# First pair of a recurrent cross attention with a gated MLP: steps 4 to 27 reordered, the next tile's integers behind the sine, its distance behind the gate product, the first layer one step ahead

## The chip, the cores and the metric

The kernel runs on one core of a Trainium2 chip. That core has five engines which run their own instruction queues in order and wait for each other by semaphores: TensorE (matrix products, PE in the profile, PEld for its weight loads), VectorE (DVE), ScalarE (ACT), GpSimd (POOL), and SyncE (SP), which here only issues DMA transfers. The metric is the device time of one execution in microseconds, the median of several runs.

## The reference

Eight batches of an attention block feed a two-layer network. All computation is in 32-bit floats; the weights arrive as 64-bit floats and are converted in the kernel.

```python
# x: (8, 8, 512, 64), state: (8, 8, 32, 64)
scores = scale * np.matmul(x, state.transpose(0, 1, 3, 2))
a = softmax(scores);   xread = np.matmul(a, state)
scores2 = scale * np.matmul(state, x.transpose(0, 1, 3, 2))
a2 = softmax(scores2); sread = np.matmul(a2, x)
y = np.concatenate([xread, sread], axis=2)
x = y.transpose(0, 2, 1, 3).reshape(8 * 544, 512)
h = x @ w_in                 # w_in 512 x 2048
g = h * np.cos(h)
out = g @ w_out              # w_out 2048 x 512
```

## The kernel before, in words

The time axis of the program is a list of tiles (`all_tiles`, from `tiles()`), and one tile is handled in one **step**. A tile is 128 of the 2048 columns of the hidden layer for the 512 tokens of one batch; so a batch has NF = 16 tiles, a pair of batches PERIOD = 32. Steps 0 to 27 go through `first_pair`, all others through `later_pair`. The order of instructions on every engine is the order in which these functions write them (`tc.manual_schedule()`); there is no planner.

A tile goes through five stages, each with a line of its own in the profile:

- `hidden` (L493): two products of 128x512 on TensorE (four matrix instructions in the trace) fill one of two PSUM banks. The bank is free again once the tile two before it has been through its last stage. The weights of this layer are the product of the attention's state and w_in, which is why the attention's read never appears as a matrix of its own: `products` (L328) forms it for four tiles at a time, and `products_kept` (L464, ScalarE) copies it to `sw`.
- `gate` (L563): ScalarE rounds the hidden value to **integers**.
- `gate2` (L566): VectorE takes the **distance** from them.
- `gate3` (L569): ScalarE takes the **sine** of that, which is the cosine of the hidden value.
- `gate4` (L583): VectorE multiplies it with the hidden value, the **gate product**, and writes it to a slot of `g_all`, which is kept in quads of four tiles. `quads_free` lists the quads that may be written.

The second layer of the first batch is `first_product` and `second_product` (`product`, L637): tile i's gate product times a 128x256 block of w_out, at step 4 + i for the first eight tiles and at every second step from 13 on for the other eight. Their sums are taken out of PSUM by `keep_bank` (L602, ScalarE) and `plus` (L606, VectorE) with the last product of each.

Between these stages every step has other work of the same engines. It is listed by `plan(b)` in six lists, of which the step's part is `todo[0]` to `todo[5]`, and written by `go(n)`: `go(0)` on TensorE, `go(1)` and `go(2)` on ScalarE, `go(3)` and `go(4)` on VectorE, and `go(5)` for the exponentials of a block after the first two. In steps 0 to 15 it is the attention of batch 1, in steps 16 to 31 that of batch 2: turns of the tokens (L287 and L296, later L310), scores (L328), maxima (L341, L357), spreads (L347), shift (L362), exponentials (L366, L373, with a table load before and after), norm (L402), turns (L408, L413), reads (L428) and their keeping (L438, L444, L449).

Three more kinds of work are tied to the steps:

- `convert(i, parts)` turns 64-bit weights into 32-bit ones, one load of 1 MB in the steps listed in `conv_at` (0 to 8 and 11 to 15): part 1 (L243) and 2 (L246) on ScalarE, b (L249) and c (L252) on VectorE, d (L257) on GpSimd; f issues a later load (L212) on SP's queue.
- `weights_at` and `idle_at` hold sums of quarters of w_out for the faster products of all later batches: `weight_sum` (L1119, VectorE), `pool_sum` (L1155) and `inner_weights` (L684, GpSimd), which are sent to DRAM on SP's queue (`send_raw`, L672, and `send`, L687) and fetched again into a ring of four blocks (`fetch_block`, L703).
- `outer_at` and `mid_at` hold differences of gate products between the batches of a pair (`outer_sum`, `sub`, L712), on VectorE or GpSimd; `Product.sums` (L712) and `sw_sums` (L526) on GpSimd prepare the later products (`Product.stage`, L765) and the later hidden layers (`seven_part`, L543).

In `first_pair` the five stages of one tile are written in one step, with the other work between them:

```python
hidden(t); go(0); gate(t); gate2(t); go(1); go(3)
gate3(t); go(5); gate4(t); go(2); go(4)
```

so that on ScalarE a tile's sine stands behind its integers and whatever `go(1)` adds, and on VectorE its product behind its distance and whatever `go(3)` adds. The products of the second layer are written at the end of the step.

Of the kernel before, what the change touches and what calls it, by code (L numbers as in the profile page):

```python
# [13 lines left out]
ALU = mybir.AluOpType  # L14
# [8 lines left out]
def kernel(  # L23
# [616 lines left out]
    def first_product(pr, i):  # L640
        product(a11, g_all[:, QT * quads_of[0, 0][i // QT] + i % QT], i)
        if i == NH - 1:
            pr.u = Held()
            for ch in range(2):
                keep_bank(pr.u, ch)

    def second_product(pr, i):
        product(a12, g_all[:, QT * quads_of[0, 1][i // QT] + i % QT], i)
        if i == NH - 1:
            o = Held()  # L650
            for ch in range(2):
                plus(o, ch, acc[ch], pr.u)
            store(2 * pr.n, 0, o)

# [253 lines left out]
    def tiles():  # L908
        pr = None
        for b in range(B):  # L910
            if b % 2 == 0:
                pr = Pair(b // 2)
            for f in range(NF):
                t = Tile()
                t.b, t.f, t.pair = b, f, pr
                t.phase, t.i = b % 2 * 2 + f // NH, f % NH
                t.row = pr.n, t.phase
                t.n, t.kn = S, 2
                t.paired = b > 1
                t.at = 1 - f // 2 % 2  # L920
                c = slice(P * f % WC, P * f % WC + P)
                t.lhs = lambda i, b=b, nt=P * f // WC, c=c: (
                    sw_of[b, nt][:, i, c])
                t.rhs = lambda i, b=b: aT_of[b][:, i]
                yield t
# [52 lines left out]
    def plan(b):  # L978
# [57 lines left out]
        if b == 0:  # L1036
            pe[0].append((0, "products", 0, SIDE, HC, WC))
            y_dve[0] += [(0, "products_taken", 0, SIDE, HC, WC),
                         (0, "inverse2")]
            prod(7, 0, 2, SIDE)  # L1040
            prod(11, 0, 3)
            prod(13, 1, 0, SIDE)
# [21 lines left out]
    for i, t in enumerate(all_tiles):  # L1064
        t.mate = all_tiles[i ^ 1]
    pairs = [all_tiles[2 * NF * n].pair for n in range(B // 2)]
    stage_at, sums_at, outer_at, mid_at, weights_at = [
        defaultdict(list) for _ in range(5)]
    idle_at = defaultdict(list)
# [26 lines left out]
    for n in range(B // 2):  # L1096
        end = n == B // 2 - 1
        for r, engine, o, x1, x2, half in (
                ((25, 26), dve, 0, 2, 0, 0),
                ((27, 28) if n else (25, 25), dve if n else pool, 0, 2, 0, 1),  # L1100
                ((31, 31), pool, 2, 3, 2, 0), ((33, 33), dve, 0, 3, 0, 0),
# [4 lines left out]
            for i in range(2):  # L1106
                at_ = (mid_at if n == 0 and r[0] == 25 and engine is dve
                       else outer_at)
                at_[PERIOD * n + r[i]].append(
                    (engine, n, o, x1, x2, half, i))  # L1110
# [33 lines left out]
    for steps, o, x1, x2, op in (  # L1144
            ((18, 19), A21, A11, A21, ALU.subtract),
            ((23, 23), SQ, A12, A22, ALU.subtract)):
        for i in range(2):
            (idle_at if o == SQ and i == 0 else weights_at)[steps[i]].append(
                lambda o=o, x1=x1, x2=x2, op=op, i=i: weight_sum(
                    o, x1, x2, op, i))  # L1150
# [6 lines left out]
    for at_, what in (  # L1157
# [9 lines left out]
            (22, lambda: inner_weights(4, matrix(A22), temps[1])),  # L1167
            (23, lambda: quads_free.append(A11)),
            (24, lambda: inner_weights(6, matrix(SQ), temps[0])),
            (25, lambda: quads_free.append(A21)),  # L1170
# [22 lines left out]
    def go(n):  # L1193
        for p in todo[n]:
            part(*p)

    def first_pair(step, t):
        last, conv = conv_at.get(step - 1, -1), conv_at.get(step, -1)
        if step == 4:
            warm(1, acc[0])  # L1200
        if step != 1:
            hidden(t)
        if step == 0:
            hidden(all_tiles[1])
# [4 lines left out]
            convert(4, "1")  # L1209
            go(0)  # L1210
        else:
            go(0)
            if step == 3:
                load_now(H)
            if step == 5:
                states(1, side_banks[0])
            gate(t)
            gate2(t)
            if step == 3:
                warm(4, acc[0])  # L1220
                part(0, "products", 1, SIDE)
            go(1)
            go(3)
            for what in mid_at[step]:
                outer_sum(*what)
            if step == 1:
                convert(4, "bcdf")
            elif last >= 0 and step < 5:
                convert(last, "bcdf")
            if conv >= 0 and not todo[1]:  # L1230
                convert(conv, "1")
        gate3(t)
        go(5)
        if step == 3:
            part(0, "products_kept", 1, SIDE)
        gate4(t)
        if step == 6:
            states_kept(1, side_banks[0])
        if last >= 0 and 4 < step < 11:
            convert(last, "bcdf")  # L1240
# [10 lines left out]
        if step > 10 and conv >= 0 and todo[1]:  # L1251
            convert(conv, "bcdf")

    def later_pair(step, t, ahead):
# [43 lines left out]
    for step, t in enumerate(all_tiles):  # L1298
# [29 lines left out]
        if t.b < B - 1 and t.b > 1 and s in (12, 13):  # L1328
            halves(t.b + 1, s - 12)
        if 4 <= step < 4 + NH:  # L1330
            first_product(pairs[0], step - 4)
        if 13 <= step < 13 + 2 * NH and not even:
            second_product(pairs[0], (step - 13) // 2)
        if step == 24:
# [44 lines left out]
```

## Time and profile before

| | |
|---|---|
| median of 3 runs | 742.84 us (742.52 to 743.03) |
| the profiled execution | 745.45 us, of it 743.7 us span |
| TensorE busy | 714.4 us, 96% of the span |
| GpSimd busy | 544.8 us, 73% |
| VectorE busy | 500.1 us, 67% |
| ScalarE busy | 338.2 us, 45% |
| clock granted to TensorE | 0.992 on average |
| step 4, hidden layer starts | 43.62 us |
| step 28, hidden layer starts | 149.28 us |

A time in the text is in microseconds from the start of the span of the profiled execution. A row of the timeline gives start, duration, engine, line, operation, output and inputs, and in brackets the idle time of the engine before it and what ended that. Steps 4 to 27 lie between 43.6 and 149.3 us.

### The profile page before, as it was taken

How to read it: one execution, taken by the hardware profiler on the slowest of the kernel's cores; microseconds unless marked ns; L12 is line 12 of the kernel's file. 1: busy time of each engine (PE TensorE's matmuls, PEld its weight loads, DVE VectorE, ACT ScalarE, POOL GpSimd, SP SyncE). 2: the span in 40 equal slices, each digit the busy share in tenths (PEclk: the TensorE clock that was granted, in tenths of full speed). 3: DMA queues.
4: the chain of work that ended last, by engine and by line, in shares of the span. 5: the costliest groups of instructions: out<-in, count | busy, mean ns of one | idle time of the engine just before them, and what ended most of it. 6: DMA issues, size and time to landing. Idle time of an engine off the chain costs nothing.

```text
span 743.7 us, 10756 instructions
## 1 busy us (share of the span) xinstructions
PE 714.4 (96%) x3624; PEld 520.3 (70%) x3624; DVE 500.1 (67%) x707; ACT 338.2 (45%) x560; POOL 544.8 (73%) x532
## 2 busy tenths in 40 slices
PE   8999889799999999999999999999999999999997
PEld 3343333367767878777777778777688788888886
DVE  4879789966965658759767587869756457355550
ACT  3777874534373446344633454443734433211110
POOL 1345569996998997497998765779989665799600
PEclk9999999899999999999999999999999999999999
DMA  8496399966245864692337834772225465456662
GB/s 252 136 265 223 124 243 304 325 137 162 79 128 115 212 151 138 142 195 84 86 86 143 184 86 112 145 170 71 73 75 122 114 201 140 113 155 198 160 152 43
DMA packets 212470, 112.39 MB, mean 151 GB/s; under 512 B 158336, under 2 KB 175232, under 8 KB 212416
## 3 DMA queue, kind: packets, MB, share of 16 engines
q1 hardware_dynamic: 211328, 111.19, 58.7%
q8 instruction: 29, 0.48, 0.3%
q10 hardware_dynamic: 960, 0.39, 0.2%
q14 instruction: 25, 0.20, 0.1%
q0 software_dynamic: 128, 0.13, 0.1%
HBM read 88.08 MB, written 23.59 MB: 150 GB/s over the span
## 4 chain that ended last, share of the span: by engine, by line
PE 60%; POOL 22%; DVE 8%; ACT 4%; issue 3%; DMA 2%; SPq 1%; DVEq 0%; POOLq 0%; ACTq 0%
PE o L765 29%; POOL g_all L712 16%; PE h L543 13%; PE h L493 7%; POOL swS_all L526 3%; PE at L328 3%; PE at L866 2%; PE at L428 2%; POOL sw L526 2%; DVE g_all L1119 1%; DVE q_all L566 1%; PE o L941 1%; PE o L866 1%; DVE i L341 1%; DVE g_all L712 1%
## 5 line engine op out<-in xcount | busy, mean ns | idle before, releaser
L712 POOL TENSOR_TENSOR g_all<-g_all 128x512 f32<-128x512 f32 x260 | 343.0, 1350 | 55.9 <-DVE g_all L712 40.7
L765 PE MATMUL o<-g_all 128*128 128x256 f32 x1456 | 344.1, 381 | 2.4 <-POOL g_all L712 2.4
L765 PEld LDWEIGHTS o<-g_all 128*128 128x128 f32 x1456 | 273.6, 190 | 49.5 <-issue 5.4
L566 DVE TENSOR_TENSOR q_all<-q_all,h 128x1024 f32<-128x1024 int32 (+1 forms) x88 | 85.5, 972 | 49.5 <-ACT q_all L563 49.3
L563 ACT ACTIVATE q_all<-h 128x1024 int32<-128x1024 f32 (+1 forms) x88 | 73.2, 832 | 81.1 <-PE h L543 35.1
L569 ACT ACTIVATE q_all<-q_all,halfpi 128x1024 f32<-128x1024 f32 (+1 forms) x88 | 84.2, 957 | 50.1 <-DVE q_all L566 50.0
L583 DVE TENSOR_TENSOR g_all<-h,q_all 128x1024 f32<-128x1024 f32 (+1 forms) x88 | 85.7, 974 | 26.5 <-ACT q_all L569 24.7
L552 DVE TENSOR_TENSOR h<-h,sums_all 128x256 f32<-128x256 f32 x96 | 41.2, 430 | 76.1 <-PE h L543 58.2
L493 PE MATMUL h<-aT,sw 128*128 128x512 f32 x128 | 63.4, 620 | 11.2 <-DVE g_all L583 10.5
L543 PE MATMUL h<-aT,sw 128*128 128x256 f32 x192 | 59.6, 392 | 3.8 <-DVE g_all L583 3.4
L543 PE MATMUL h<-aS_all,swS_all 128*128 128x256 f32 x192 | 60.2, 395 | 2.6 <-ACT sums_all L547 1.8
L543 PE MATMUL h<-aS_all,sw 128*128 128x256 f32 x192 | 58.0, 384 | 0.1
L712 DVE TENSOR_TENSOR g_all<-g_all 128x1024 f32<-128x1024 f32 x38 | 54.4, 1449 | 0.1
L493 PEld LDWEIGHTS h<-aT,sw 128*128 128x128 f32 x128 | 23.4, 194 | 44.1 <-issue 21.1
L543 PEld LDWEIGHTS h<-aS_all,swS_all 128*128 128x128 f32 x192 | 33.9, 189 | 27.0 <-issue 11.3
L770 ACT COPY o<-o 128x256 f32<-128x256 f32 x26 | 9.3, 357 | 85.5 <-PE o L765 85.5
L257 POOL TENSOR_TENSOR w_in<-w_in,aS_all 128x1024 int32<-128x1024 int32 (+1 forms) x10 | 19.3, 1929 | 38.0 <-DVE w_in L252 23.8
L543 PEld LDWEIGHTS h<-aT,sw 128*128 128x128 f32 x192 | 34.5, 189 | 16.3 <-DVE g_all L583 12.2
L526 POOL TENSOR_TENSOR swS_all<-sw 128x128 f32<-128x128 f32 x48 | 22.5, 469 | 30.8 <-ACT sw L464 30.8
L543 PEld LDWEIGHTS h<-aS_all,sw 128*128 128x128 f32 x192 | 35.6, 190 | 8.2 <-DVE h L552 2.7
L776 ACT COPY o<-sums_all 128x256 f32<-128x256 f32 x26 | 9.8, 378 | 68.9 <-PE o L765 68.9
L606 DVE SCALAR_TENSOR_TENSOR held<-o,held 128x512 f32<-128x512 f32 x40 | 27.2, 681 | 13.7 <-PE o L765 13.1
(116 smaller groups left out, 923.2 us busy)
## 6 DMA issues: line engine op xcount, KB each, us to landing
g_all<-blocks_kept SPq DMA_DIRECT2D x206, 256.0 KB, 2.9
blocks_kept<-g_all SPq DMA_DIRECT2D x48, 256.0 KB, 3.7
g_all<-in_moe_w_out_dram SPq DMA_DIRECT2D x8, 1024.0 KB, 5.1
out_dram<-ot SPq DMA_DIRECT2D x128, 64.0 KB, 2.1
g_all<-in_moe_w_in_dram SPq DMA_DIRECT2D x6, 1024.0 KB, 5.4
xT<-in_x_dram SPq DMA_DIRECT2D x96, 64.0 KB, 3.0
x_b<-in_x_dram SPq DMA_DIRECT2D x24, 256.0 KB, 4.7
x_b<-in_x_dram SPq DMA_DIRECT2D x16, 128.0 KB, 4.3
```

The lines of the kernel that those rows point to most:

```text
L328: nc.tensor.matmul(out=(to or at)[j][Ns * k:Ns * k + Ns, n0:n1], lhsT=w[D * j:D * j + D, self.b, Ns * k:Ns * k + Ns], rhs=r(slice(D * j, D ...
L493: nc.tensor.matmul(out=t.hp, lhsT=t.lhs(i), rhs=t.rhs(i), start=(i == 0), stop=(i == t.kn - 1))
L526: nc.gpsimd.tensor_tensor(o, x1, x2, op=op)
L543: nc.tensor.matmul(out=out_, lhsT=w, rhs=r, start=start, stop=True, skip_group_check=True)
L552: nc.vector.tensor_tensor(o, h2[:, LO], sums_all[:, 0], op=ALU.add)
L563: nc.scalar.activation(t.q.bitcast(I32), t.hp, func=ACTF.Copy, bias=0.25)
L566: nc.vector.tensor_tensor(t.q, t.q.bitcast(I32), t.hp, op=ALU.subtract)
L569: nc.scalar.activation(t.q, t.q, func=ACTF.Sin, bias=halfpi, scale=-TWO_PI)
L583: nc.vector.tensor_tensor(g, t.hp, t.q, op=ALU.mult)
L606: nc.vector.scalar_tensor_tensor(out=out.t[:, ch], in0=bank, scalar=TWO_PI, in1=b.t[:, ch], op0=ALU.mult, op1=ALU.add)
L712: engine.tensor_tensor(o[:, i:i + n], x1[:, i:i + n], x2[:, i:i + n], op=ALU.subtract)
L765: nc.tensor.matmul(out=o, lhsT=ring[(self.first + k) % NB][:, i], rhs=g[:, i], start=(start and i == 0), stop=(i == QT - 1), skip_group_ch ...
```

## The change

The change concerns `first_pair` and what is placed in its steps.

- From step 4 to step 26 a step writes the hidden layer of the tile after its own (`coming`), and the products of the second layer directly behind it, ahead of `go(0)`. The products' last parts are split off as `first_kept` and `second_kept`.
- The step's own sine (`gate3`) is followed at once by the next tile's integers (`gate(coming)`), and its own gate product (`gate4`) by the next tile's distance (`gate2(coming)`). The other work of ScalarE and VectorE comes after these.
- In a step with exponentials of a later block (`todo[5]`, step 23) the next tile's sine and product are also written, ahead of the exponentials; the step after leaves them out (`t.g` is set).
- The attention's side products of steps 7 and 11 move to 6 and 10, and both go to the side banks. The states of the other four batches (`states(1, ...)`) are turned at step 4, not 5, and copied at step 5, not 6.
- The second half of a weight sum (SQ) moves from step 23 to 25, `inner_weights(6)` from 24 to 25, and GpSimd's outer sums from 25 to 24, so that on GpSimd the outer sums stand ahead of the inner weights; VectorE's outer sums of steps 25 and 26 move from the middle of the step (`mid_at`) to its end. The quad A11 may be written from step 22.

```diff
     def first_product(pr, i):
         product(a11, g_all[:, QT * quads_of[0, 0][i // QT] + i % QT], i)
-        if i == NH - 1:
-            pr.u = Held()
-            for ch in range(2):
-                keep_bank(pr.u, ch)
+
+    def first_kept(pr):
+        pr.u = Held()
+        for ch in range(2):
+            keep_bank(pr.u, ch)
 
     def second_product(pr, i):
         product(a12, g_all[:, QT * quads_of[0, 1][i // QT] + i % QT], i)
-        if i == NH - 1:
-            o = Held()
-            for ch in range(2):
-                plus(o, ch, acc[ch], pr.u)
-            store(2 * pr.n, 0, o)
...
-            prod(7, 0, 2, SIDE)
-            prod(11, 0, 3)
+            prod(6, 0, 2, SIDE)
+            prod(10, 0, 3, SIDE)
...
-                ((27, 28) if n else (25, 25), dve if n else pool, 0, 2, 0, 1),
+                ((27, 28) if n else (24, 24), dve if n else pool, 0, 2, 0, 1),
...
-                at_ = (mid_at if n == 0 and r[0] == 25 and engine is dve
-                       else outer_at)
-                at_[PERIOD * n + r[i]].append(
+                outer_at[PERIOD * n + r[i]].append(
...
-            ((23, 23), SQ, A12, A22, ALU.subtract)):
+            ((23, 25), SQ, A12, A22, ALU.subtract)):
...
-            (23, lambda: quads_free.append(A11)),
-            (24, lambda: inner_weights(6, matrix(SQ), temps[0])),
+            (22, lambda: quads_free.append(A11)),
+            (25, lambda: inner_weights(6, matrix(SQ), temps[0])),
...
+    AHEAD = 4
+
+    def first_products(step):
+        if 4 <= step < 4 + NH:
+            first_product(pairs[0], step - 4)
+        if 13 <= step < 13 + 2 * NH and not even:
+            second_product(pairs[0], (step - 13) // 2)
+
+    def first_products_kept(step):
+        if step == 3 + NH:
+            first_kept(pairs[0])
+        if step == 11 + 2 * NH:
+            second_kept(pairs[0])
+
     def first_pair(step, t):
         last, conv = conv_at.get(step - 1, -1), conv_at.get(step, -1)
+        coming = all_tiles[step + 1] if AHEAD <= step < PERIOD - 5 else None
         if step == 4:
             warm(1, acc[0])
-        if step != 1:
+        if step != 1 and step <= AHEAD:
             hidden(t)
+        if coming is not None:
+            hidden(coming)
+            first_products(step)
         if step == 0:
             hidden(all_tiles[1])
             warm(3, acc[0])
...
             gate2(t)
             convert(3, "bcdf")
             convert(4, "1")
-            go(0)
-        else:
-            go(0)
-            if step == 3:
-                load_now(H)
-            if step == 5:
-                states(1, side_banks[0])
+        go(0)
+        if step == 4:
+            states(1, side_banks[0])
+        if 0 < step <= AHEAD:
             gate(t)
             gate2(t)
             if step == 3:
+                load_now(H)
                 warm(4, acc[0])
                 part(0, "products", 1, SIDE)
+        if 0 < step < AHEAD:
             go(1)
             go(3)
-            for what in mid_at[step]:
-                outer_sum(*what)
             if step == 1:
                 convert(4, "bcdf")
-            elif last >= 0 and step < 5:
+            elif last >= 0:
                 convert(last, "bcdf")
             if conv >= 0 and not todo[1]:
                 convert(conv, "1")
-        gate3(t)
-        go(5)
+        early = coming is not None and todo[5]
+        if t.g is None:
+            gate3(t)
+        if coming is not None:
+            gate(coming)
         if step == 3:
             part(0, "products_kept", 1, SIDE)
-        gate4(t)
-        if step == 6:
+        if t.g is None:
+            gate4(t)
+        if coming is not None:
+            gate2(coming)
+        if early:
+            gate3(coming)
+            go(3)
+            gate4(coming)
+        go(5)
+        if step >= AHEAD:
+            go(1)
+            if not early:
+                go(3)
+            if conv >= 0 and not todo[1]:
+                convert(conv, "1")
+        if step == 5:
             states_kept(1, side_banks[0])
-        if last >= 0 and 4 < step < 11:
+        if coming is not None:
+            first_products_kept(step)
+        if last >= 0 and AHEAD <= step < 11:
             convert(last, "bcdf")
         if conv >= 0 and todo[1] and step > 0:
             convert(conv, "1")
...
         go(4)
         if step > 10 and conv >= 0 and todo[1]:
             convert(conv, "bcdf")
+        if coming is None and step >= AHEAD:
+            first_products(step)
+            first_products_kept(step)
...
-        if 4 <= step < 4 + NH:
-            first_product(pairs[0], step - 4)
-        if 13 <= step < 13 + 2 * NH and not even:
-            second_product(pairs[0], (step - 13) // 2)
```

More of the change, by code (lines that the diff above doesn't have):

```diff
@@ L641, in first_product, with second_kept @@
         product(a11, g_all[:, QT * quads_of[0, 0][i // QT] + i % QT], i)
-        if i == NH - 1:
-            pr.u = Held()
-            for ch in range(2):
-                keep_bank(pr.u, ch)
+    def first_kept(pr):
+        pr.u = Held()
+        for ch in range(2):
+            keep_bank(pr.u, ch)
     def second_product(pr, i):
         product(a12, g_all[:, QT * quads_of[0, 1][i // QT] + i % QT], i)
-        if i == NH - 1:
-            o = Held()
-            for ch in range(2):
-                plus(o, ch, acc[ch], pr.u)
-            store(2 * pr.n, 0, o)
+    def second_kept(pr):
+        o = Held()
+        for ch in range(2):
+            plus(o, ch, acc[ch], pr.u)
+        store(2 * pr.n, 0, o)
     ORDER = (0, 4, 5, 1, 6, 2, 3)
@@ L914, in tiles @@
                 t = Tile()
-                t.b, t.f, t.pair = b, f, pr
+                t.b, t.f, t.pair, t.g = b, f, pr, None
                 t.phase, t.i = b % 2 * 2 + f // NH, f % NH
@@ L1066 @@
     pairs = [all_tiles[2 * NF * n].pair for n in range(B // 2)]
-    stage_at, sums_at, outer_at, mid_at, weights_at = [
-        defaultdict(list) for _ in range(5)]
+    stage_at, sums_at, outer_at, weights_at = [
+        defaultdict(list) for _ in range(4)]
     idle_at = defaultdict(list)
```

## The prediction

> **What bounds the kernel now.** The clock and span first: TensorE was granted 0.992 on average, so the span is not a throttled one. Then the busy shares by stretch. After about 140 us TensorE is 95 to 100% busy almost to the end, so a later stage gives back little and loses little: what the first pair ends with, TensorE carries to the end. The open time is in steps 0 to 27. In the table below the columns are sum of the stretch, then busy us and instructions of PE, PEld, DVE, ACT, POOL, then TensorE's clock, DMA share and GB/s.
>
> ```profile
> 72.00:106.00 34.00, 28.14 (x136) 11.17 (x134) 27.51 (x40) 29.72 (x45) 17.81 (x10) 1.00 0.66 179
> 106.00:130.00 24.00, 23.22 (x89) 8.40 (x90) 20.61 (x28) 10.45 (x16) 23.69 (x19) 1.00 1.06 301
> ...
> 135.00:140.00 5.00, 1.25 (x2) 0.50 (x2) 4.93 (x7) 1.81 (x3) 4.52 (x4) 0.75 1.02 339
> 140.00:145.00 5.00, 5.00 (x21) 2.55 (x20) 4.60 (x6) 3.06 (x5) 5.00 (x4) 0.57 1.04 269
> ```
>
> See three things: from 72 to 106 ScalarE is the fullest engine; from 106 on GpSimd and the DMA engines are full and VectorE nearly; and at 135 to 140 TensorE stands almost still and then runs at half clock. The waits (engine, line, what it waited for: us in total, times, longest) say which hand-over is late between 45 and 150 us:
>
> ```profile
> ACT q_all L569 <- DVE q_all L566: 21.8, 18, 3.5
> ...
> PE h L493 <- DVE g_all L583: 9.5, 9, 3.7
> ...
> DVE q_all L566 <- ACT q_all L563: 8.4, 9, 2.4
> DVE g_all L583 <- ACT q_all L569: 8.0, 12, 0.9
> ```
>
> The sine waits for the distance, and the hidden layer for the product that frees its bank. The largest case is tile 24, in VectorE's and ScalarE's order of time:
>
> ```profile
> 128.94 0.69 DVE L583 TENSOR_TENSOR g_all<-h,q_all 128x512 f32<-128x512 f32 x1 [0.79 <-ACT q_all L569]
> 129.55 2.33 DVE L1119 TENSOR_TENSOR g_all<-g_all 128x1024 f32<-128x1024 f32 x1
> ...
> 133.02 2.30 DVE L1119 TENSOR_TENSOR g_all<-g_all 128x1024 f32<-128x1024 f32 x1
> 135.25 0.67 DVE L566 TENSOR_TENSOR q_all<-q_all,h 128x512 f32<-128x512 int32 x1
> ...
> 138.32 0.65 DVE L583 TENSOR_TENSOR g_all<-h,q_all 128x512 f32<-128x512 f32 x1
> ```
>
> Tile 24's product ends behind the second attention block's exponentials (ScalarE 128.9 to 132.7, two table loads) and two weight sums. TensorE's hidden layer of tile 26 waits 3.75 us for it, and starts at 139.03.
>
> **What the Trainium skill says.** "TensorE: Matmul & The Clock Gate", Part 1, puts the array at half clock after an idle window of about 3.4 us, and says that the windows run freely. The trace agrees: idle from 135.28, clock 0.50 from about 137.8 to 144.2, and the hidden layer at 139.03 takes 3.78 us, not 1.72. "ScalarE: Activation LUTs", What ACT_TABLE_LOAD costs, gives 1283 ns a load and a drain of about 1380 ns with it; the trace has loads of 1.28 us, and shows no drain (the sine of 128.19 ends at 128.91, the load starts at 128.93). "SBUF — State Buffer", Who interferes with whom, lets a VectorE operation with two SBUF inputs and a GpSimd one that reads exclude each other. The weight sum of L1119 took 2.05 to 2.33 us beside a busy GpSimd, and the same shape in L712 1.45 on average, so I keep 2.2 for it.
>
> **The change part by part.** The recipe: I lay the new instruction order of each engine out by hand with durations of this trace. Start to start, where the next one waits: hidden to integers 2.05 (105.99, 108.07), integers to distance 0.63, distance to sine 0.71, sine to product 0.76, product to hidden 0.75. Back to back: hidden or product pair on TensorE 1.72, sine 0.63, integers 0.48, each conversion on ScalarE 1.04, gate operation on VectorE 0.60, its conversion pair 0.70 and 1.20.
>
> *Steps 4 to 9.* From 43.62 to 68.87 TensorE had 12 hidden or first-layer products (20.6) and 4.4 of turns, states and side products, 25.0 in 25.25 us: nothing to win. The new order costs ScalarE: keep2's copy (L449) now follows two hidden tiles and a product, and comes at 49.5 instead of 46.0 with two conversions behind it; a token copy waits 0.9, a side copy 0.5. It gains where the sine of tile 9 waited 3.19. Laid out, the sine of tile 8 starts at 65.4 (before 66.1), of tile 9 at 68.6 (71.6), of tile 10 at 78.2 (78.1), since the exponentials between still wait for VectorE. Sum: 0.
>
> *Steps 10 to 16.* ScalarE was idle 3.85 us before its sines (1.56, 0.28, 1.04, 0.97); these go. Side products, turns and reads, though, stand behind the hidden tile ahead, which waits for the product two tiles back. At step 13 hidden 14 waits until 88.3, then product 1.7 and side product 1.25: its copy (L464) starts at 93.0 while ScalarE is free at 90.8, and both conversions stand behind it: 2.2 lost. Moving the side products from 7 and 11 to 6 and 10 avoids two more such waits. Laid out: sine 12 at 85.5 (86.8), 14 at 96.05 (95.8), 15 at 99.25 (100.2), the last conversion on VectorE at 103.05 to 104.25 (102.6 to 103.85). Sum: 0.4 us late for GpSimd, which from there on is full.
>
> *Steps 17 to 23.* VectorE sets the pace in both orders (20.6 busy of 24). Laid out, tile 20's product starts at 119.65 (120.1), tile 22's at 126.0 (125.7), tile 23's at 128.4 (128.9): 0.5 us won.
>
> *Steps 23 to 28.* Here tile 24's sine and product are put ahead of the exponentials: product at 130.9 (138.32). Hidden 26 no longer waits. Then exponentials until 134.8, integers of 25, two side copies, a table load, sine 25 at 137.5; VectorE has one weight sum, sums, distance, transpose and norm, and product 25 comes at 139.6 (142.5). Hidden 27 starts at 140.35 after some 3.0 us of TensorE idle. The second weight sum and both outer sums (2.2, 1.65 and 1.75) now lie behind distances 26 and 27, where product 26 pays for them: 144.65 (145.9), product 27 at 147.6 (149.05). TensorE: hidden 27 1.72, reads 2.05, product 1.72, so hidden 28 at 145.9 (149.28), hidden 29 at 148.7 (152.11), hidden 30 at 152.85 (155.66). **Won at that point: 2.8 us.**
>
> *Queues moved past.* GpSimd's four outer sums go ahead of the last inner weights (L684). These now wait for the second weight sum at 143.0, where GpSimd arrives at 140.3: a new wait of 2.7 against 1.16 before; behind it come the first product's sums (5.6) and swS (L526). That gives swS at 154.6 (before 154.82); TensorE read it at 157.81, less 2.8 is 155.0: it just fits. On SP's queue the three ring fetches now precede eight weight sends; the reads of step 14 come at 95.5 (91.2), so the token loads behind them and the stretch of full DMA (91.6 to 149) start 4.3 late. The first ring block, issued at 141.5 before and needed at 153.9, still goes out by 142 to 144 and lands in 4: hidden. The outer keep and plus steps split from the products (L602, L606) cost nothing while ScalarE and VectorE have the slack above; with it gone, 1.0 and 1.3 us. Later GpSimd idles 4.99 us at 176 to 181, which lets it catch up, and nothing after step 28 differs.
>
> The sum: the profiled execution took 745.45, its span 743.7 and 1.75 around it. Less 2.8: 742.65. The median of the runs is 2.61 below the profiled one, so **740.0 us**.
>
> Unknowns with both ends: the clock after the idle of 3.0 us falls (before it fell after some 2.5 us of idle) or holds: costs 0 to 2.6, the latter being half of 5.2 us at half clock before; laid out with it, 1.8 of the 2.8 go. I take 0, as the idle is shorter, and keep both. VectorE's and GpSimd's exclusion on the moved sums: 0.7 a sum, four sums, so up to 2.8 lost, or as much gained where they no longer meet.
>
> **The rivals.** *The clock falls anyway*: 1.0 won, 741.8. For it: idle of 3.0 against 2.5; against it: freely running windows. *ScalarE fills up in steps 10 to 16*: the 3.85 come through because side copies are less late than laid out, and GpSimd starts as much earlier: 2.8 + 3.85, 736.2. For it the 21.8 us before the sines; against it the full TensorE until 72 and VectorE's 27.5 of 34. *Slower, by the place of the side work on TensorE*: its copies hold ScalarE up by 1.5, 0.9, 0.5, 2.2 and 0.5 at steps 4, 5, 6, 13 and 16, 5.6 together. If the removed sine waits do not pay them back, because VectorE's products come too late for the hidden tiles, the conversions end 5.6 late, GpSimd and DMA with them, and the change costs 5.6 - 2.8: 745.6. It decides once the last conversion ends more than 2.8 later than at 103.85. *No effect*: the gain is eaten by the new wait of the inner weights and by late swS; 742.8.
>
> **How the numbers follow.** 0.2% is 1.5 us, about what a measurement of this kernel can tell from no change. Chances: the layout 0.36, ScalarE fills 0.10, clock falls or no effect 0.23, slower 0.31. Faster 0.46, same 0.23, slower 0.31. The range goes from 736.0 to 746.5; the likeliest case alone has 738 to 741.3.
>
> **What would show it.** Right: in the changed profile the waits of the sine for the distance nearly vanish before 150 us; tile 24's product starts before the exponentials; hidden 28 starts near 146; GpSimd waits near 140 for the weight sum; ScalarE waits for TensorE before L464. Wrong: the last conversion later than 106 us, hidden 28 later than 149, or idle of TensorE after 150 us that was not there before.

## The result, and the profile after

The changed kernel takes **746.94 us** (median of 4 runs, 746.37 to 747.19), the kernel before on the same chip 742.93 (742.52 to 743.48): a ratio of **1.0052, 95% interval 1.0035 to 1.007**. It is 4.0 us slower; forecast were 740.0. The execution shown here took 746.37 us, its span 744.6, at a clock of 0.996.

First the same stretches as before (columns: sum of the stretch, then busy us and instructions of PE, PEld, DVE, ACT, POOL, TensorE's clock, DMA share, GB/s):

```profile
72.00:106.00 34.00, 25.64 (x118) 10.93 (x117) 29.69 (x40) 27.82 (x40) 17.89 (x9) 1.00 0.57 173
106.00:130.00 24.00, 21.29 (x91) 8.03 (x90) 20.03 (x30) 11.34 (x19) 22.04 (x16) 1.00 1.02 278
...
135.00:140.00 5.00, 4.08 (x16) 2.08 (x14) 4.15 (x7) 4.97 (x10) 5.00 (x5) 1.00 1.01 318
140.00:145.00 5.00, 2.85 (x4) 1.17 (x4) 5.00 (x5) 2.00 (x4) 3.85 (x3) 0.69 1.02 347
```

From 72 to 106 us TensorE does 25.6 us of work where it did 28.1 before: 2.5 us of it are late by then. VectorE, not ScalarE, is now the fullest engine there. The open time near 135 has moved to 140, and the clock still falls. The waits between 45 and 150 us (us in total, times, longest) answer to the four lines shown of before:

```profile
PE h L493 <- DVE g_all L583: 12.9, 10, 3.1
DVE g_all L583 <- ACT q_all L569: 11.6, 8, 3.9
...
ACT q_all L569 <- DVE q_all L566: 7.8, 10, 1.4
ACT sw L464 <- PE h L328: 6.3, 4, 2.1
DVE q_all L566 <- ACT q_all L563: 5.8, 6, 2.4
...
ACT aS_all L246 <- POOL w_in L257: 2.2, 1, 2.2
```

The sine's wait for the distance fell from 21.8 to 7.8 as the change intends. Three waits stand in its place: the gate product now waits for the sine (11.6, longest 3.9, against 8.0 and 0.9), ScalarE's copy L464 waits for TensorE's side product, and the conversion L246 waits 2.2 us for GpSimd. The hidden layer's wait, which is what costs, grew from 9.5 to 12.9.

The gate products tell where it happens. To take out different starts, I compare with a second profile of the kernel before (e1 below), whose step 4 starts at 42.58, the changed kernel's at 42.67. Product 6 comes at 56.26 (e1: 55.58), **product 7 at 63.33 (60.56)**, product 9 at 74.06 (71.54), 16 at 107.50 (104.09), 23 at 129.80 (126.80), 24 at 132.40 (135.87), 28 at 153.50 (151.17), and 33 at 187.63 (185.30). So 2 to 3 us are lost at one tile, up to 3.4 by step 16; tile 24 is 3.5 us early, and by tile 28 the kernel is 2.3 late again, which TensorE carries to the end. The two profiled executions end 2.7 us apart (spans 744.6 and 741.9); the medians are 4.0 apart, as e1's execution lies 0.7 above its median and this one 0.6 below.

ScalarE around sine 7 in the changed kernel (start, duration, engine, line, operation; idle time before in brackets):

```profile
56.13 0.58 ACT L563 ACTIVATE q_all<-h 128x512 int32<-128x512 f32 x1
58.57 1.07 ACT L464 COPY sw<-h 128x512 f32<-128x512 f32 x2 [1.86 <-PE h L328]
59.53 0.61 ACT L296 COPY xT<-at 128x512 f32<-128x512 f32 x1
60.00 1.17 ACT L243 ACTIVATE w_in<-g_all 128x1024 f32<-128x1024 f32 x1
61.05 0.60 ACT L296 COPY xT<-at 128x512 f32<-128x512 f32 x1
61.51 1.17 ACT L246 ACTIVATE aS_all<-g_all 128x1024 int32<-128x1024 uint32 x1
62.55 0.74 ACT L569 ACTIVATE q_all<-q_all,halfpi 128x512 f32<-128x512 f32 x1
```

In e1 the sine stood directly behind L464:

```profile
58.53 1.06 ACT L464 COPY sw<-h 128x512 f32<-128x512 f32 x2
59.48 0.74 ACT L569 ACTIVATE q_all<-q_all,halfpi 128x512 f32<-128x512 f32 x1
60.10 1.18 ACT L243 ACTIVATE w_in<-g_all 128x1024 f32<-128x1024 f32 x1
```

L464 ends at the same time in both. But the new order writes a tile's sine at the head of its own step, behind all other work of the step before, here 3 us of token copies and conversions. Its distance had been there since 57.5. VectorE passes the lateness on:

```profile
58.18 1.22 DVE L252 SCALAR_TENSOR_TENSOR g_all<-g_all 128x1024 int32<-128x1024 int32 x1
63.33 0.69 DVE L583 TENSOR_TENSOR g_all<-h,q_all 128x512 f32<-128x512 f32 x1 [3.92 <-ACT q_all L569]
...
65.76 0.65 DVE L249 TENSOR_SCALAR w_in<-w_in 128x1024 int32<-128x1024 int32 x1
66.44 1.23 DVE L252 SCALAR_TENSOR_TENSOR w_in<-g_all,w_in 128x1024 int32<-128x1024 int32 x1
...
70.75 2.19 DVE L252 SCALAR_TENSOR_TENSOR w_in<-g_all,w_in 128x1024 int32<-128x1024 int32 x1
```

In e1 VectorE came to product 7 and to load 10's conversion without a wait:

```profile
60.56 0.65 DVE L583 TENSOR_TENSOR g_all<-h,q_all 128x512 f32<-128x512 f32 x1
61.14 0.67 DVE L249 TENSOR_SCALAR w_in<-w_in 128x1024 int32<-128x1024 int32 x1
```

While VectorE waits 3.9 us for the sine, load 10's conversions (L249, L252), whose data ScalarE has delivered by 61.2 (the end of L243), stand behind the product; they come at 65.76 (e1: 61.14). From 63.3 VectorE then works without a gap, GpSimd gets load 10 at 67.81 (63.21), and ScalarE's conversion of load 12, which writes the same one of two buffers, waits for that:

```profile
70.20 1.18 ACT L246 ACTIVATE aS_all<-g_all 128x1024 int32<-128x1024 uint32 x1 [2.23 <-POOL w_in L257]
```

### The profile page after: what moved, and what is told of

It is laid out like the page before. It is cut to its first block, busy times and chain, and to the rows that moved or that the text cites. A ratio compares the mean times of both kernels' runs of the same rounds, so it can differ in the third digit from the quotient of the medians.

```text
span 744.6 us, 10767 instructions
## 1 busy us (share of the span) xinstructions
PE 711.0 (95%) x3624; PEld 518.5 (70%) x3624; DVE 499.9 (67%) x707; ACT 338.0 (45%) x560; POOL 545.2 (73%) x532
## 4 chain that ended last, share of the span: by engine, by line
PE 59%; POOL 21%; DVE 10%; issue 4%; ACT 3%; DMA 2%; SPq 1%; DVEq 0%; POOLq 0%; ACTq 0%
PE o L767 28%; POOL g_all L714 16%; PE h L543 12%; PE h L493 7%; POOL swS_all L526 3%; PE at L328 3%; PE at L868 2%; PE at L428 2%; POOL sw L526 2%; DVE g_all L583 1%; DVE q_all L566 1%; PE o L943 1%; PE o L637 1%; PE o L868 1%; DVE xT L310 1%
## 5 line engine op out<-in xcount | busy, mean ns | idle before, releaser
L257 POOL TENSOR_TENSOR w_in<-w_in,aS_all 128x1024 int32<-128x1024 int32 (+1 forms) x10 | 19.2, 1925 | 41.8 <-DVE w_in L252 28.6
L778 ACT COPY o<-sums_all 128x256 f32<-128x256 f32 x26 | 9.8, 377 | 68.6 <-PE o L767 68.6
```

## The experiments

Every time is a median, with the ratio to the kernel before on the same chip (median 742.80 for e1 to e4, 742.50 for e5 to e8, 742.61 for e9 to e11, 742.37 for e12 to e14, 742.83 for e15 to e17). The cuts of code are abridged. Where times of different profiles are compared "from product 1", the start of tile 1's gate product (33.38 in the changed kernel, 33.29 in e1) is taken off, so that different starts drop out.

### Which steps lose

e1 is the kernel before, unchanged.

> The kernel before, unchanged. Theory CLOCK (the profiled execution of before was 2.6 us above its median because it caught half clock at 138 to 144 us and a cold start, which its usual runs do not have): most spans here are near 741 us, mean clock 0.995 or more, and a profile without the half clock shows hidden 28 some 3.5 us earlier than 149.3. Theory ORDER (the profile shown is typical, and all of the loss comes from the new order): spans near 743.7, clock 0.992, half clock at 138 to 144 again.

742.96 us, 1.0004 (0.9995 to 1.0013). Its profile, too, has half clock (0.56 at 135 to 140), but starts step 4 a microsecond earlier than the one that the prediction was made from, and is another 1.2 us ahead by tile 19. The profile of before was an untypical execution by that much. CLOCK is right in part: of the 12 executions seven were granted 0.999 or 1.0 and took 742.3 on average, five 0.994 to 0.996 and took 743.7. ORDER's spans near 743.7 were not seen.

e2, e3: the new order in a part of the steps only, with the moves that belong to it.

```diff
-        first_pair(step, t)
+        (new_pair if A0 <= step <= A1 else old_pair)(step, t)   # e2: 17, 27   e3: 4, 16
```

> Old order up to step 16, the new one from step 17 on, with all moves that belong to it (outer sums, weight sum, last inner weights, tile 24 ahead of the exponentials). If the loss lies in steps 4 to 16 (ORDER), this is 740 to 743. If the second half loses too (idle before hidden 27 and half clock, later weight sum), it is 744 to 747. Laid out in the prediction: 2 to 3 us below before as it was profiled, that is about level with a usual run of before.

743.57 us, 1.0013 (1.0006 to 1.002), between the two expectations. Its trace has a loss that the changed kernel does not have, at the seam. Step 17 writes two hidden layers with nothing between them; TensorE stands 2.35 us before the second, and its clock falls to 0.50 from 106 to 109 us:

```profile
104.76 2.77 PE L493 MATMUL h<-aT,sw 128*128 128x512 f32 x4 [2.35 <-DVE g_all L583]
```

Product 19 comes 83.15 us after product 1 (e1: 79.53, changed kernel: 83.98, of which 3.3 were lost before step 17).

> New order in steps 4 to 16 alone, old order and old places from step 17 on. If the loss lies here, 746 to 748: the last conversion on VectorE ends 3 us later than in before, and everything after it too. If it lies in the second half, 742 to 744.

746.62 us, 1.0054 (1.0042 to 1.0066). **Steps 4 to 16 alone lose as much as the whole change**; the part that was to win, steps 17 to 27, shows no gain in the medians, neither in e2, which has the seam's loss in it, nor in the changed kernel against e3.

e4: before, with steps 23 and 24 alone in the new order (A0, A1 = 23, 24), that is with tile 24's hidden layer, sine and product ahead of the exponentials; the outer sums and weight sums stay where they were, and quad A11 may be written a step earlier.

> The kernel before, with one part of the change: at step 23 the hidden layer, sine and product of tile 24 stand ahead of the exponentials. ORDER: hidden 26 no longer waits 3.75 us; 2 to 3 us faster, 740 to 741. CLOCK: usual runs of before lose little there, so 742 to 743.5.

745.24 us, 1.0037 (1.0024 to 1.0049), outside both expectations. Moving tile 24 forward alone costs 2.4 us: in the trace TensorE still stands before its reads (2.01 us, for L413) and before hidden 26 (0.83), and hidden 26 still runs at half clock (3.78 us).

### Side work of TensorE, ScalarE's conversions, the buffer

e5: in steps 5 to 16 `go(0)` goes ahead of the next tile's hidden layer. e6: conversion "1" (L243) goes ahead of the side copies. e7: a third buffer for load 12. e8: all three.

```diff
+        if 4 < step <= 16:                    # e5
+            go(0)
         if coming is not None:
             hidden(coming)
...
         if step >= AHEAD:
+            if conv >= 0:                     # e6
+                convert(conv, "1")
             go(1)
...
         e = low[i % 2][:, c0:c0 + m * w]
+        if i == 12:                           # e7
+            e = quad(3).rearrange("p t s -> p (t s)")[:, 0:m * w]
```

> The changed kernel, but in steps 5 to 16 the side work on TensorE (turns, scores, side products, reads) stands ahead of the next tile's hidden layer instead of behind it. Theory SIDE (its copies hold ScalarE up, 6.3 us before L464, 1.0 before L449, 0.9 before L296): ScalarE's waits before L464 shrink by 4 or more and 1.5 to 3.5 us of the loss come back, 743.5 to 745.5. Theory BUFFER (the wait of L246 for GpSimd at step 8, 2.2 us, and VectorE behind it): 746 to 747.5. Theory HIDDEN (the integers, one tile ahead, wait for TensorE's hidden layer, 15.0 us, which waits for the product two tiles back): no gain or a loss, 746.5 to 749.

754.14 us, 1.0155 (1.0124 to 1.0186): worse by another 7 us, outside all three expectations. TensorE in e5:

```profile
57.79 1.93 PE L328 MATMUL h<-w_in,st_all 64*32 64x512 f32 x8 [3.19 <-POOL w_in L257]
```

The side product that the change moved from step 7 to 6 reads a w_in that GpSimd converts just then. Ahead of the hidden layer it makes that wait too, and the wait takes the clock down as well (0.50 from 58 to 60 us; the same product took 1.06 in the changed kernel). Putting all side work forward is no remedy; putting forward only the other side work was not tried.

> The changed kernel, but from step 4 on the first conversion of a step (L243) stands right behind the next tile's integers on ScalarE, ahead of the copies of the attention. SIDE: the waits for TensorE are then spent in converting; the last conversion ends 2 to 3 us earlier and 743.5 to 745.5 results. BUFFER: 746 to 747.5. HIDDEN: 746 to 747.5.

745.25 us, 1.0031 (1.0018 to 1.0044), in SIDE's range: 0.21 of the 0.52% come back. The two intervals overlap, but the trace says the same: product 16 comes 72.02 us after product 1, in the changed kernel 74.12. Conversion "1" now fills the time in which ScalarE waited for TensorE in front of L464.

> The changed kernel, but the low halves of load 12 (step 8) go to a free quad, so that its second conversion (L246) does not wait for GpSimd to have read the buffer of load 10. BUFFER: the 2.2 us wait goes, and 1.5 to 2.2 us of the loss with it: 744.7 to 745.5. SIDE and HIDDEN: the sine of tile 9 comes 2 us earlier, but the exponentials still wait for VectorE (L362, L357): under 0.7 us, 746.2 to 747.

746.05 us, 1.0049 (1.0034 to 1.0064): no more than the intervals leave open, and between the two expectations. Product 16 comes 74.14 us after product 1, as in the changed kernel (74.12). The 2.2 us wait of L246 is gone from the trace, but the exponentials (L366) then wait 1.87 us for VectorE. The buffer wait is a sign of the lateness, not its cause.

> The three edits of the other runs together. If SIDE and BUFFER make up the loss of the first half: 741 to 743.5, level with before or better. HIDDEN: most of the loss stays, 745 to 747.

752.84 us, 1.014 (1.0124 to 1.0155), outside both expectations: e5's loss remains.

### The place of the sine

On top of e6. e9: the side copies of steps 4 to 6 go behind the sine of the tile ahead; e10: those of steps 4 to 15. e11: old order to step 6, new from 7. In e11 the side product, moved to step 6 in the old order, overwrites the bank with the states of the other four batches before they are copied; all instructions are still there.

```diff
-            go(1)                             # e9, e10: at the end of step s
+        gate3(t)                              # at the head of step s + 1
+        for p in todo_kept:                   # todo[1] of step s
+            part(*p)
...
-        first_pair(step, t)                   # e11
+        (new_pair if step >= 7 else old_pair)(step, t)
```

> On top of the kernel that converts "1" ahead of the side copies (745.25): the side copies of steps 4, 5 and 6 (L449, L296, L464) stand on ScalarE behind the sine of the tile ahead (L569) and not in front of it. QUEUE (ScalarE runs in order, and the copies, which wait 0.28, 0.38 and 1.15 us for TensorE there, hold up a sine whose distance has long been there): sine 7 starts near 59.5 and not at 61.7, tile 7's product near 60.3 instead of 62.5 (before 60.6), and 1.5 to 2 us come back: 743.3 to 743.8. FULL (TensorE is full from 44 to 62 us, so an earlier product lets no hidden layer start earlier, and the later copies hold up the integers): no gain, 745 to 746.

748.27 us, 1.007 (1.0058 to 1.0083). Both theories missed. Sine 7 came at 60.48 (e6: 61.71, from a start 0.8 us later), so little was won, and on TensorE:

```profile
61.71 3.63 PE L493 MATMUL h<-aT,sw 128*128 128x512 f32 x4 [2.79 <-ACT sw L464]
```

Hidden 8 reads what L464 copies. Since the change issues it a step ahead, the copy is now on its path at once, and hidden 8 pays for the delay of L464: 2.79 us of waiting, and then half clock (0.50 from 62 to 65 us), so that it took 3.63 us and not 1.88. Behind the sine L464 costs more than the sine's place brings.

> The same for the side copies of steps 4 to 15 (also the L464 of steps 10 and 13, the L413, L471 and L473 copies of the turns and reads, and L602). QUEUE: what e9 gives, and the 0.56 at step 10 and 2.15 us of step 13 in which ScalarE waits for TensorE before L464 no longer hold up a sine: 742.3 to 743.3. FULL: as e9 or worse, 745 to 747, since attention copies come later and TensorE's reads wait for them.

749.06 us, 1.0092 (1.0074 to 1.011): the same, outside both.

> The order of the kernel before up to step 6 (with the side product in step 6), the new order with conversion "1" ahead of the side copies from step 7 on. QUEUE (the loss that is left at 745.25 arises in steps 4 to 6, where ScalarE waits for TensorE in front of a sine): tile 7's product near 61.5, 743.3 to 744. VECTOR (it arises in steps 7 to 16, where each tile's product stands behind the VectorE work of the step before): 745 to 745.5.

746.71 us, 1.0058 (1.0046 to 1.007): outside both. With the side product in step 6 of the old order its L464 stands ahead of sine 6, which comes at 59.09 (e1: 54.83). So the product's move from 7 to 6 costs in the old order too; this run doesn't tell the theories apart.

### VectorE's order in step 7

e12, on top of e6: VectorE's conversions of load 10 go ahead of tile 7's product, into the gap. e13 adds sine 7 directly behind L464. e14 adds six matmuls, whose result nobody reads, ahead of hidden 27.

```diff
+        if step == 7:                         # e12
+            convert(last, "bcdf")
         if t.g is None:
             gate4(t)
...
+            if step == 6:                     # e13
+                part(*todo[1].pop(0))         # L464
+                gate3(coming)
             go(1)
...
+        if step == 26:                        # e14: 6, e16: 3
+            for _ in range(6):
+                nc.tensor.matmul(out=side_banks[0], lhsT=ident, rhs=w_in[:, 0, 0:S], ...)
         if coming is not None:
             hidden(coming)
```

> On top of the kernel that converts "1" ahead of the side copies (745.25): in step 7, VectorE's conversions of load 10 (L249, L252, 1.9 us, then GpSimd's L257) stand ahead of tile 7's product, in the 3.1 us in which VectorE waits for sine 7, and not behind it, distance 8 and L341. VECTOR (the late sine 7 is passed on because VectorE is then full without a gap from 64 to 77 us and load 10's GpSimd conversion comes at 67.5 and not at 63.2): L257 of load 10 near 62.5, ScalarE's 2.1 us wait of L246 for it gone, tile 9's product near 71.5 to 72 instead of 73.8, 743.2 to 744. TENSOR (TensorE's side product, its copy L464 and hidden 8 behind it set the pace of steps 6 to 9, whatever VectorE does): product 9 at 73 or later, 745 to 745.5.

**742.70 us, 1.0004 (0.9994 to 1.0014)**: the loss is gone; VECTOR holds, and 0.5 us better than its bound. VectorE and GpSimd in e12:

```profile
58.63 0.69 DVE L249 TENSOR_SCALAR w_in<-w_in 128x1024 int32<-128x1024 int32 x1
59.35 3.27 DVE L252 SCALAR_TENSOR_TENSOR w_in<-g_all,w_in 128x1024 int32<-128x1024 int32 x1
62.54 0.68 DVE L583 TENSOR_TENSOR g_all<-h,q_all 128x512 f32<-128x512 f32 x1
...
70.93 0.68 DVE L583 TENSOR_TENSOR g_all<-h,q_all 128x512 f32<-128x512 f32 x1
```

```profile
58.85 2.68 POOL L257 TENSOR_TENSOR g_all<-g_all,aS_all 128x1024 int32<-128x1024 int32 x1 [1.95 <-DVE g_all L252]
62.76 2.38 POOL L257 TENSOR_TENSOR w_in<-w_in,aS_all 128x1024 int32<-128x1024 int32 x1 [1.23 <-DVE w_in L252]
```

Product 7 is no earlier than in e6 (62.54 and 62.47, where e6's profile starts 0.7 us later), yet load 10 reaches GpSimd at 62.76 and not at 67.54, L246 no longer waits, and product 9 comes at 70.93 (e6: 73.78; e1: 71.54). What was lost in step 7 was a place in VectorE's queue, not the sine as such.

> e12, and on ScalarE in step 6 sine 7 stands directly behind L464, ahead of two token copies (L296) and of L246 (together 2.0 us). Hidden 8 gets its L464 as early as before, so that it does not wait as in e9. VECTOR: sine 7 near 59.7 and not 61.7, product 7 near 61.3 (behind the two conversions); what is left of the lateness of steps 4 to 9 goes, up to 0.7 us more: 742.5 to 743.5. TENSOR: as e12 or 0.3 later, since the token copies and L246 come 0.7 later.

742.87 us, 1.0005 (0.9996 to 1.0013), which fits both expectations. Sine 7 comes at 58.70 (e12: 61.05), and nothing follows from it: product 7 stands behind the conversions.

> e13, and six matmuls of 128x512 into a side bank ahead of hidden 27, which fill part of TensorE's 3 us of idle time there. CLOCK (the idle time takes the clock to 0.5, and hidden 27 then takes 3.6 us and not 1.8): the clock stays at 1.00 from 139 to 146, hidden 27 takes 1.9, and 0.8 to 1.8 us come back: 741 to 742.5. ELSEWHERE (hidden 27 and 28 wait for VectorE's sums all the same): the clock stays up but the time is that of e13, within 0.3.

743.07 us, 1.0005 (0.9997 to 1.0014). The clock stays at 1.00, but the six matmuls ran from 134.71 to about 139.9 and held hidden 27 up by what the clock gave. The number is ELSEWHERE's, but it settles nothing.

### One cause or two, and the clock

e15: e12's edit alone, on the changed kernel. e16: e12 with three such matmuls. e17: the kernel before with three ahead of hidden 26.

> The changed kernel with nothing but VectorE's conversions of load 10 (L249, L252) ahead of tile 7's product in step 7; conversion "1" stays behind the side copies. ONE CAUSE (both edits act on the same lateness, that of load 10 on GpSimd, so the earlier of VectorE's two queue places is enough): 743 to 744. TWO CAUSES (ScalarE's side copies in front of the conversions cost 1.7 us on their own, VectorE's order 2.5): 744.2 to 744.8.

745.44 us, 1.0035 (1.0024 to 1.0047), outside both expectations. VectorE in e15:

```profile
61.10 1.28 DVE L249 TENSOR_SCALAR w_in<-w_in 128x1024 int32<-128x1024 int32 x1 [1.78 <-ACT w_in L243]
62.41 1.22 DVE L252 SCALAR_TENSOR_TENSOR w_in<-g_all,w_in 128x1024 int32<-128x1024 int32 x1
63.55 0.68 DVE L583 TENSOR_TENSOR g_all<-h,q_all 128x512 f32<-128x512 f32 x1
```

Without e6's edit, ScalarE delivers L243 only at 61, behind L464. Of the 0.52%, e6 brings 0.21, e15 0.17 and both together 0.48 (e12); the intervals, some 0.13% to each side, leave open whether the two add up. The traces settle it. Start of the gate products in us from product 1:

| | product 9 | 16 | 23 | 28 | 33 |
|---|---|---|---|---|---|
| kernel before (e1) | 38.25 | 70.80 | 93.51 | 117.88 | 152.01 |
| changed kernel | 40.68 | 74.12 | 96.42 | 120.12 | 154.25 |
| e6, ScalarE's conversion first | 39.52 | 72.02 | 94.32 | 117.90 | 152.11 |
| e15, VectorE's conversions first | 38.53 | 71.97 | 94.28 | 118.08 | 152.22 |
| e12, both | 37.34 | 69.85 | 92.13 | 115.88 | 150.01 |

At product 16, e6 is 2.1 us ahead of the changed kernel, e15 2.15, and e12 4.27: the two gains add up, so there are two causes, as TWO CAUSES has it. e15's lies in step 7. e6's lies half at its start (1.2 by product 9) and half in steps 10 to 16 (0.9), where the changed kernel's conversion at step 13 stands behind an L464 that waits 2.15 us for TensorE. That e15's median is above TWO CAUSES' range is not explained: its trace is 2.0 us ahead of the changed kernel's at product 33, its span only 0.9 shorter.

> e12, and three matmuls of 128x512 (2.7 us) into a side bank ahead of hidden 27: half of e14's, where they ran until 139.9 us and held hidden 27 up from 138.06 to 139.86. CLOCK: hidden 27 starts near 138.1 at clock 1.00 and takes 1.9 us, hidden 28 starts near 143.7 instead of 145.3, and 1 to 1.6 us are won: 741.0 to 741.9. ELSEWHERE (what follows waits for VectorE's product 26 near 142 or later and for its sums): 742.4 to 743.

742.36 us, 1.0001 (0.9992 to 1.0011). TensorE in e16:

```profile
137.63 1.99 PE L493 MATMUL h<-aT,sw 128*128 128x512 f32 x4 [0.47 <-DVE g_all L583]
...
143.26 1.88 PE L493 MATMUL h<-aT,sw 128*128 128x512 f32 x4
...
153.21 0.70 PE L543 MATMUL h<-aS_all,swS_all 128*128 128x256 f32 x2 [0.69 <-POOL swS_all L526]
```

CLOCK's steps happen: hidden 27 takes 1.99 us (e12: 3.12), and hidden 28 starts 2.1 us earlier than e12's 145.33. Then it is given back: product 28 is 1.1 us ahead (148.34 and 149.47), the first read of swS waits 0.7 us for GpSimd, product 33 is 0.5 ahead (183.06 and 183.60), and both spans are 740.6. Of each of these leads 0.4 is an earlier start, so that 0.1 is left at product 33. The time is ELSEWHERE's.

> The kernel before with the same three matmuls ahead of hidden 26, where TensorE waits 3.4 us for tile 24's product. CLOCK: hidden 26 takes 1.9 and not 3.8 us, and the executions near 743.4 go: 740.5 to 741.5. ELSEWHERE: 742.2 to 742.8, the clock being 1.00.

742.69 us, 0.9998 (0.999 to 1.0007). Hidden 26 took 1.99 us at full clock instead of 3.78, and then hidden 27 waited 1.05 us for product 25. The median is ELSEWHERE's. But the execution shown kept what the clock gave: product 33 comes 150.71 us after product 1, 1.3 earlier than in e1, whose clock fell. That the median doesn't show it fits with most executions of the kernel before having the clock anyway: of the 27 on this chip 18 were granted 0.998 or more, as were all 13 here.

No version here beats the kernel before beyond the measurement: e12 and e16 equal it.

## Why the prediction was wrong, point by point

**Steps 4 to 9, "Sum: 0": wrong, and the main step that failed.** They lost 2.4 us: product 9 comes 40.68 us after product 1, in e1 38.25. The prediction's time axis starts 0.95 us later at step 4 (43.62 against 42.67), so 0.95 is added to the changed kernel's times here. Sine 8 was laid out at 65.4 and came at 66.65, sine 9 at 68.6 and came at 72.2. I put a side copy's delay at step 6 at 0.5 us; L464 waited 1.86. And I never laid out load 10: that its conversions on VectorE (L249, L252) stand behind product 7, which waits for sine 7, was not in the sum. Their place carries 2.15 us (e15 against the changed kernel), ScalarE's copies ahead of L243 another 1.2 (e6, product 9); with both mended product 9 comes 0.9 earlier than in e1 (e12), which is what the rest of the order gains there. The end of the chain, GpSimd's L257 and L246's wait for it, is not what costs (e7).

**Steps 10 to 16, "0.4 us late": wrong in size.** The last conversion on VectorE was laid out to end at 104.25; it ended at 107.58, that is 108.5. Of this most came in from the steps before. From product 9 to 16 it took 33.44 us, in e1 32.55: 0.9 lost, not 0.4. The term worked out for step 13 was right (2.15 us before L464, 2.2 forecast), and e6's order, which fills that wait, takes the 0.9 away (32.50).

**Steps 17 to 23, "0.5 won": about right.** From product 16 to 23 the changed kernel took 22.30 us (e6, e12 and e15 the same within 0.02), e1 22.71: 0.4 won. In e2's trace the loss lies at the seam.

**Steps 23 to 28: the order right, the times late.** Tile 24's product does start ahead of the exponentials (132.40), VectorE's sums lie where they were laid out, and the idle time ahead of hidden 27 was forecast at 3.0 and came at 3.06:

```profile
138.05 1.04 PE L408 MATMUL at<-ident,xT 128*128 128x128 f32 x8
142.15 3.56 PE L493 MATMUL h<-aT,sw 128*128 128x512 f32 x4 [3.06 <-DVE g_all L583]
```

But it started at 143.1 on the old axis, 2.75 later than laid out, and the clock fell: 3.56 us, not 1.72. I had put the fall at 0 and kept 2.6 as the bound; it was 1.8. "TensorE: Matmul & The Clock Gate", Part 1, names an idle window of about 3.4 us; here the clock fell after 3.06, so an idle time a little under the window was no ground for taking the better end. Nor did the trace of before agree with that figure, as I wrote: its clock fell less than 2.5 us into the idle time (0.76 on average from 137 to 138 us, idle from 135.28). Together the late start and the clock make 4.6 us; hidden 28, at 149.36 or 150.3 on the old axis, missed 145.9 by 4.4. From product 23 to 28 the changed kernel won 0.7 us on e1 (23.70 and 24.37); 2.9 were forecast between product 23 and hidden 28. With the full clock at that place the gain is not simply kept: e16's is gone by product 33.

**"The median is 2.61 below the profiled one, so 740.0": wrong.** Of the 2.61, 0.95 was a later start, which a layout inherits. Another 1.1 arose in steps 17 to 19 (e1), a stretch that the layout had just replaced, so that part of it was counted twice. The changed kernel's profiled execution lies 0.57 below its median. This step cost 2.61 - 0.95 + 0.57 = 2.2 of the 6.9 us.

**The queues.** GpSimd's new wait of the inner weights was forecast at 2.7 and took 1.16, as before. "swS just fits" was right, with nothing to spare: once e16 took time off TensorE's path, the read of swS waited (0.69 us).

**The rivals.** The slower one named the mechanism's entrance, side copies that wait on ScalarE for TensorE, and its deciding point (the last conversion over 2.8 later than 103.85) was passed. Its 745.6 was 1.3 short, and as near as that by luck: it had 5.6 us lost by the last conversion and 2.8 won after it, the traces have 3.3 lost by product 16 and 1.1 won from there to product 33; the rest of the 4.0 is mostly how far the profiled executions lie from their medians. Its cause was half right: ScalarE's conversions behind copies that wait for TensorE make up half of the loss at product 16 (2.1 us, e6), VectorE's order in step 7 the other half (2.15, e15); and the one other place tried for TensorE's side work was worse (e5). ScalarE did not fill up in steps 10 to 16 (27.8 busy of 34, 29.7 before); the clock did fall.

What stays open: which part after product 33 takes back half of e15's lead, and why e12, which by its profile is 2.0 us ahead of e1 at product 33, has no better median than the kernel before. In e1's execution the clock fell for longer than in e12's, but by how much the medians differ in that no trace shows.

## What to carry to other kernels

When an order is laid out by hand, follow every engine that shares a queue with the moved work up to the point where its data are used again, also those that aren't moved: here load 10 was harmed by standing behind a product that waited. If an instruction waits for another engine, put work whose data are there ahead of it; and once one queue is mended, look for the same fault in the next: here ScalarE's and VectorE's order lost 2.1 us each, and mending one left the other. A single profiled execution should not be shifted to the median by a constant before a second profile has shown where the difference lies.

## What the runs showed of the hardware

- An L252 on VectorE (two inputs in SBUF) that started while GpSimd was in L257 took 3.27 us instead of 1.23 (e12: from 59.35 to 62.62; L257 ended at 61.53). In the changed kernel one took 2.19 behind GpSimd's L686, which ended at 71.86. In both it ended 1.08 to 1.09 us after GpSimd's instruction, so it seems to have stood until then and to have run nearly in full after it. "SBUF — State Buffer", Who interferes with whom, says that a VectorE instruction with two SBUF inputs contends with a GpSimd one that reads SBUF, and that the port pair they share is an exclusive lock; this agrees. I had expected a fraction (0.7 us a sum).
- TensorE's clock fell after 3.06 us of idle time (0.69 on average from 140 to 145), and three matmuls of 2.7 us together in that gap kept it at 1.00 in the profiled execution (e16). The length of the gap alone does not decide: one of 2.77 us ahead of hidden 11 (74.8 us) left the clock at 1.00 in the changed kernel, and the same gap ahead of the same layer took it to 0.50 in e6 (76 to 78 us); in e2 2.35 us were enough.
